# Attention and channel mix on one core: batch 5's output transposed by DMA, two tail loads moved ahead of a weight, fewer filler matmuls, and new written-out orders

## The chip, the cores and the metric

The kernel runs on one core of a Trainium2 chip. Its time is that of one execution on the device in microseconds (us), the median of three runs: 228.89 us before the change (228.83 to 229.37). The engines are named as in the profile: PE is TensorE's matmuls and PEld its weight loads, DVE is VectorE, ACT is ScalarE, POOL is GpSimd and SP is SyncE. POOL and SP issue transfers here, and POOL's convert float32 to bfloat16 on the way.

## The reference

Two layers follow each other. The first is causal attention with a linear distance bias and a window of 128 tokens, for 8 batches, 8 heads, 576 tokens and a head size of 64. The second mixes each token with the one before it and applies a gated, squared-ReLU feed-forward with 512 features and 1024 hidden ones.

```python
# attention, per batch and head
scores = q @ k.T / sqrt(64)
mask = (rel >= 0) & (rel < 128)            # rel = query position - key position
attn = softmax(where(mask, scores - slope[h] * |rel|, -1e9))
x[:, heads side by side] = attn @ v
# channel mix
xk = mu_k * x + (1 - mu_k) * x_prev        # x_prev: the token before
xr = mu_r * x + (1 - mu_r) * x_prev
out = sigmoid(xr @ w_r) * ((relu(xk @ w_k) ** 2) @ w_v)
```

## The kernel before

**Attention.** The work is cut by batch `b` (0 to 7) and by group `g` of two heads (0 to 3). q and k must stand with the head dimension on the partitions. For batches 0 to 3 PE transposes them through PSUM, and ACT or DVE copies the result to `qk` (`qk_quad`, `qk_some`). For batches 4 to 7 (`XB`) SP issues eight transposing DMAs per batch, `qx<-cb` (`flip`). The 64 tokens behind the last full block of 128 are the tail: q's and k's go to `ts` and, transposed, to `tt`; v's go to `tv`. Scores (`scores`) are matmuls over 64 rows, with the two heads side by side in the array. Batch 0 adds the bias by a matmul of `sid` and `dist`; later batches multiply by `mask` on DVE. ACT takes the exponential into `at`. The value product (`attend`) multiplies `at` by `vs` and `tv`, whose extra column of ones gives the sum; DVE divides (`rc`) and writes `xu`.

**From attention to channel mix.** `xu` has tokens on the partitions and must be turned. PE turns it in batches 0 to 5. In batch 0 it does so by group (`out_t`). In batches 1 to 5 (`OH`) it does so for two groups at once (`out_some`): 20 small transposes into two PSUM banks, copied by ACT to `xt`. For the batches in `XO` SP issues a transposing DMA per group instead, `xt<-xu` (`out_flip`); `XO` is asked first. DVE then takes the difference of neighbouring tokens (`dl`) and makes `xk` and `xr` (`shift`).

**Channel mix.** Two batches make 1152 tokens, worked in chunks of 256, 384 or 512 (`channel_mix`). Per chunk there are eight groups of four matmuls with `wk_sb`, with ReLU on ACT and the square on DVE or ACT (`kk`). Per 128 tokens come four matmuls with `wr_sb` and a tanh on ACT (`rs`), then eight with `wv_sb`, and DVE writes `ot`, which has five buffers, and SP stores it. All matmuls are recorded at one line, L395.

**What sets the order.** A planner (`Plan`) makes a node of each piece of work. For PE, ACT and DVE the table `ORDER` says which node takes which place, so an engine runs exactly the written list and waits where a node isn't ready. SP's and POOL's orders come from the planner's modelled run. POOL loads follow `LOADS`, a string of steps: `v` and `V` are batch 0's v (blocks 0 and 1; blocks 2, 3 and the tail), `2` its second half of q and k, `t` its tails of q and k, `K` and `k` the halves of w_k, `a`, `b`, `c` batch 1, `R` w_r, `W` and `w` the halves of w_v. At the start PE runs `NWARM` matmuls of a zeroed tile (`warm`, the fillers), which also stand in the list between pieces of batch 0. The last stores are cut in two where a count of SP's and ACT's transfers, `n_hw`, isn't a multiple of 8 (`n_split`).

Of the kernel before, what the change touches and what calls it, by code (L numbers as in the profile page):

```python
# [20 lines left out]

ORDER = {
    "PE": [int(x) for x in """
# [17 lines left out]
""".split()],  # L41
    "ACT": [int(x) for x in """
# [11 lines left out]
""".split()],  # L54
    "DVE": [int(x) for x in """
# [16 lines left out]
""".split()],  # L72
}

# [168 lines left out]
def kernel(  # L243
# [14 lines left out]
    B, H, S, D = q.shape  # L258
# [15 lines left out]
    PE, ACT, DVE, POOL, SPE, FAB, VIR = "PE", "ACT", "DVE", "POOL", "SP", "FAB", "VIR"  # L274
    NQ, NA, NX, NV, NC = 4, 4, 4, 2, 2
    XB = range(4, B)
    XO = range(6, B)
    X0 = 16
    NWARM = 90
    LOADS = 'v2KtVkabRWwc'  # L280
    XD = 4
    OTL = 1.5
    FIN = 384
# [328 lines left out]
    def load_step(what):  # L612
        if what in "vV":
            if what == "v" and VCUT:
                n_w["d"] = pool_op(0.55, emit_cut, [n_ident])
            for j in ((0, 1) if what == "v" else (2, 3)):
                vl[0].append(v_load(0, j, vh[0], [gv[0]] + blank_v + (
                    src0[1, VDEP - 1] if VDEP and j == 0 else [])))
                if j == 0 and not VCUT:
                    n_w["d"] = pool_op(0.55, emit_cut, [n_ident, last[POOL]])  # L620
                    last[POOL] = n_w["d"]
            if what == "V":
                vl[0].append(tv_load(0, vh[0], blank[0:4]))
        elif what in "23":
            if what == "2":
                src1[0] = src1[1] = [run_load(lambda: part_buf, i, 0, 256, 2, 0, H) for i in range(2)]
        elif what == "t":
            th[0], tl[0] = tail_load(0)
        elif what in "Kk":
            j = int(what == "k")  # L630
            n_w["k", j] = w_load(wk_sb[:, :, 512 * j:512 * j + 512],
                                 moe_w_k[:, 512 * j:512 * j + 512], 820 + 210 * (1 - j))
        elif what == "R":
            n_w["r"] = w_load(wr_sb, moe_w_r, 840)
        elif what in "Ww":
            j = int(what == "w")
            n_w["v", j] = w_load(wv_sb[:, 4 * j:4 * j + 4], moe_w_v[512 * j:512 * j + 512], 820)
        elif what in "abc":
            batch_load(1, what)
# [33 lines left out]

    for what in LOADS:
        load_step(what)
# [32 lines left out]
    g_wm = plan.add(VIR, 0.0001, 0.0001, [], (0,), None, [h_wm])  # L708
    for i in range(NWARM):
        plan.add(PE, 0.118 if i < 40 else 0.056, 0.0, [n_warm, g_wm], (1e12, i), emit_warm, (), [h_wm])  # L710
# [277 lines left out]

    n_hw = 39 + sum(4 if g in FT else 2 for g in range(3)) + 8 * len(XB) + len(XTT) + G * len(XO)
    n_split = -n_hw % 8  # L990
# [249 lines left out]
    for b in range(1, B):  # L1240
# [4 lines left out]
        for g in range(G):  # L1245
# [21 lines left out]
            r, hx = attend(b, g, 0, NJ, ha, [m0, m1] + vl[b], prio)  # L1267
            if b in XO:
                xks[b, g], xrs[b, g] = shift(b, g, 0, S, out_flip(b, g, r, hx, xth[b]),
# [54 lines left out]
```

## Time and profile before

| | |
|---|---|
| median of three runs | 228.89 us |
| the profiled execution | 228.23 us |
| its span (first to last instruction) | 226.2 us |
| granted TensorE clock | 0.998 |
| PE busy | 218.4 us, 2572 matmuls |
| DVE busy | 186.3 us |
| ACT busy | 156.2 us |
| POOL busy | 92.1 us |

The span is about 2.0 us shorter than the execution, whose start and end lie around it. In a row of the timeline the first number is the start in us from the span's beginning, the second the length of the merged piece, then come engine, line, operation, output<-input by the program's names, shapes and a count. In brackets stands how long the engine had been idle, and what ended that. A PE piece is as long as its matmuls' pipelined ends are modelled, so rates are read from start to start. Rows of DMA issues (SPq, POOL) show the issue; the landing comes later and is told as "to landing".

### The profile page before, as it was taken

How to read it: one execution, taken by the hardware profiler on the slowest of the kernel's cores; microseconds unless marked ns; L12 is line 12 of the kernel's file. 1: busy time of each engine (PE TensorE's matmuls, PEld its weight loads, DVE VectorE, ACT ScalarE, POOL GpSimd, SP SyncE). 2: the span in 40 equal slices, each digit the busy share in tenths (PEclk: the TensorE clock that was granted, in tenths of full speed). 3: DMA queues.
4: the chain of work that ended last, by engine and by line, in shares of the span. 5: the costliest groups of instructions: out<-in, count | busy, mean ns of one | idle time of the engine just before them, and what ended most of it. 6: DMA issues, size and time to landing. Idle time of an engine off the chain costs nothing.

```text
span 226.2 us, 6452 instructions
## 1 busy us (share of the span) xinstructions
PE 218.4 (97%) x2572; PEld 132.6 (59%) x2603; DVE 186.3 (82%) x418; ACT 156.2 (69%) x284; POOL 92.1 (41%) x118
## 2 busy tenths in 40 slices
PE   8999999999999999999999999999999999999994
PEld 7766855756666555555666554556665564655442
DVE  7388979899879999988989969969989999834153
ACT  2489999899999876877497198665697644545121
POOL 8956727599971973396258610330000000000000
PEclk9999999999999999999999999999999999999999
DMA  6999999999999999999999999799811083202026
GB/s 169 180 185 199 197 195 177 224 149 155 182 171 165 98 194 173 197 170 151 206 183 128 155 188 179 155 114 239 154 31 32 36 158 64 90 3 80 17 96 229
DMA packets 129981, 33.19 MB, mean 147 GB/s; under 512 B 116632, under 2 KB 126112, under 8 KB 129952
## 3 DMA queue, kind: packets, MB, share of 16 engines
q0 software_dynamic: 95728, 16.26, 100.6%
q1 hardware_dynamic: 32480, 15.94, 33.5%
q10 hardware_dynamic: 1744, 0.59, 1.1%
q8 instruction: 20, 0.33, 0.6%
q14 instruction: 9, 0.07, 0.1%
HBM read 33.56 MB, written 9.44 MB: 190 GB/s over the span
## 4 chain that ended last, share of the span: by engine, by line
PE 78%; ACT 12%; DMA 3%; DVE 3%; issue 2%; DVEq 0%; ACTq 0%
PE duo L395 68%; PE duo L742 6%; ACT at L766 3%; PE duo L398 3%; DMA out_dram<-ot 3%; ACT qk L715 3%; ACT xt L715 2%; ACT rl L1022 2%; ACT mask L1198 1%; DVE ot L1054 1%; PE duo L748 1%; ACT kk L994 1%; DVE xu L819 1%; DVE kk L996 0%; ACT rs L1040 0%
## 5 line engine op out<-in xcount | busy, mean ns | idle before, releaser
L395 PE MATMUL duo<-xk,wk_sb 128*128 128x256 bf16 (+2 forms) x413 | 71.0, 313 | 0.5 <-ACT rl L1022 0.2
L766 ACT ACTIVATE at<-duo 128x1024 bf16<-128x1024 f32 (+2 forms) x68 | 64.4, 1008 | 8.4 <-PE duo L742 8.3
L395 PE MATMUL duo<-wv_sb,kk 128*128 128x512 bf16 (+2 forms) x279 | 68.5, 373 | 1.3 <-issue 0.6
L1022 ACT ACTIVATE rl<-duo 128x256 bf16<-128x256 f32 (+2 forms) x104 | 47.6, 499 | 26.2 <-PE duo L395 20.9
L395 PEld LDWEIGHTS <-wk_sb 128*128 128x128 bf16 x416 | 38.9, 97 | 23.8 <-issue 1.6
L779 DVE TENSOR_TENSOR at<-at,mask 128x1024 bf16<-128x1024 bf16 x56 | 37.9, 686 | 7.1 <-ACT at L766 6.7
L395 PEld LDWEIGHTS <-kk 128*128 128x128 bf16 x296 | 26.8, 98 | 27.4 <-issue 0.9
L519 POOL DMA_DIRECT2D vs<-in_v_dram x32 | 28.5, 909 | 32.5 <-PE duo L395 30.9
L996 DVE TENSOR_TENSOR kk<-rl 128x256 bf16<-128x256 bf16 (+2 forms) x92 | 29.6, 336 | 10.8 <-ACT rl L1022 10.1
L1040 ACT ACTIVATE rs<-duo 128x512 bf16<-128x512 f32 x36 | 22.3, 628 | 22.5 <-DVE ot L1054 15.1
L395 PE MATMUL duo<-wr_sb,xr 128*128 128x512 bf16 x133 | 34.9, 379 | 0.6
L1054 DVE SCALAR_TENSOR_TENSOR ot<-rs,duo 128x512 f32<-128x512 bf16 (+2 forms) x37 | 24.3, 664 | 9.3 <-PE duo L395 5.7
L819 DVE TENSOR_TENSOR xu<-duo,rc 128x640 bf16<-128x640 f32 (+2 forms) x36 | 26.6, 745 | 0.4
L913 DVE SCALAR_TENSOR_TENSOR xr<-dl,mu_sb,xt 128x576 bf16<-128x576 bf16 (+1 forms) x32 | 24.9, 779 | 0.0
L913 DVE SCALAR_TENSOR_TENSOR xk<-dl,mu_sb,xt 128x576 bf16<-128x576 bf16 (+1 forms) x32 | 24.5, 778 | 0.1
L395 PEld LDWEIGHTS <-at 128*128 128x128 bf16 x576 | 21.3, 97 | 5.5 <-issue 0.9
L395 PEld LDWEIGHTS <-xr 128*128 128x128 bf16 x144 | 13.8, 98 | 14.5 <-issue 0.4
L395 PE MATMUL duo<-vs,at 128*128 128x65 bf16 x512 | 21.8, 193 | 0.0
L550 POOL DMA_DIRECT2D cb<-in_k_dram x20 | 17.8, 930 | 4.9 <-DMA vs<-in_v_dram 4.4
L550 POOL DMA_DIRECT2D cb<-in_q_dram x20 | 17.8, 942 | 1.4 <-DMA cb<-in_k_dram 1.4
L715 ACT COPY xt<-duo 128x640 bf16<-128x640 bf16 (+3 forms) x28 | 15.6, 593 | 2.4 <-PE duo L398 2.4
L715 ACT COPY qk<-duo 128x512 bf16<-128x512 bf16 (+1 forms) x26 | 15.1, 605 | 2.6 <-PE duo L398 2.6
(73 smaller groups left out, 189.0 us busy)
## 6 DMA issues: line engine op xcount, KB each, us to landing
out_dram<-ot SPq DMA_DIRECT2D x30, 256.0 KB, 4.7
vs<-in_v_dram POOLq DMA_DIRECT2D x32, 128.0 KB, 7.9
cb<-in_q_dram POOLq DMA_DIRECT2D x20, 128.0 KB, 9.5
cb<-in_k_dram POOLq DMA_DIRECT2D x20, 128.0 KB, 10.8
out_dram<-ot SPq DMA_DIRECT2D x10, 128.0 KB, 1.8
wk_sb<-in_moe_w_k_dram POOLq DMA_DIRECT2D x2, 512.0 KB, 8.7
cb<-in_q_dram POOLq DMA_DIRECT2D x4, 256.0 KB, 8.7
cb<-in_k_dram POOLq DMA_DIRECT2D x4, 256.0 KB, 8.9
```

Source lines behind the costliest of these rows:

```text
L395: return use(h, nc.tensor.matmul(*a, **k))
L519: return dma(POOL, 256, issue_t(1024), lambda e: nc.gpsimd.dma_start(out=vs_buf[h.idx][:, j, :, 0:D], in_=v[b, :, 128 * j:128 * j + 128].r ...
L550: return [dma(POOL, 256, issue_t(1024), lambda e, r=r: nc.gpsimd.dma_start(out=cb_buf[h.idx][:, i, r], in_=src[:, :, r]), [g], kind="q") f ...
L715: return (nc.scalar.copy if e == ACT else nc.vector.tensor_copy)(out=out, in_=in_)
L766: lambda e, ah=ah, w=w, hp=hp: nc.scalar.activation(out=ah(), in_=two(hp)[:, :, 0:w], func=AF.Exp, scale=float(scale)), (), [hp])
L779: nc.vector.tensor_tensor(out=a, in0=a, in1=m, op=ALU.mult)
L819: use(hp, nc.vector.tensor_tensor(out=out_, in0=a5()[:, :, :, 0:D], in1=rc[:, :, 0:nt, None].to_broadcast([128, 2, nt, D]), op=ALU.mult), hx)
L913: lambda e: nc.vector.scalar_tensor_tensor(out=buf[hk.idx][:, g, e0 + c0:e0 + c1], in0=dls(), scalar=mu[:, g:g + 1], in1=xc(1), op0=ALU.mu ...
L996: nc.vector.tensor_tensor(out=out, in0=in_, in1=in_, op=ALU.mult)
L1022: a = op(ACT, act_t(n), [s], pr, lambda e, hp=hp, hr=hr: use(hp, nc.scalar.activation(out=rl_buf[hr.idx][:, 0:n], in_=one(hp)[:, 0:n], fun ...
L1040: lambda e, hp=hp, hs=hs: use(hp, nc.scalar.activation(out=rs_buf[hs.idx], in_=one(hp), func=AF.Tanh, scale=0.5), hs), [hs], [hp])
L1054: use(hv, nc.vector.scalar_tensor_tensor(out=ot_buf[ho.idx][:, a:b], in0=rs_buf[hs.idx][:, a:b], scalar=1.0, in1=one(hv)[:, a:b], op0=ALU. ...
```

## The change

`XO` takes batch 5 in, so that its four groups are turned by four transposing DMAs from SP, and 40 small transposes on PE and four copies on ACT are no longer there. The step `t` stands ahead of `K`. `NWARM` is 82 instead of 90. `n_hw` rises by four, so that one late store is cut in two instead of five. The lists for PE, ACT and DVE are new from end to end; of them only the beginnings are shown.

```diff
 ORDER = {
     "PE": [int(x) for x in """
-40 113 74 125 85 56 118 80 117 109 43 51 42 89 121 63 103 88 49 92 96 66 94 48 119 127 126 68 100 55 101 110 107
...
+84 109 92 74 83 70 64 40 43 115 97 106 59 80 62 102 110 47 81 100 50 65 105 91 117 103 60 77 93 49 79 112 72 63
...
     XB = range(4, B)
-    XO = range(6, B)
+    XO = range(5, B)
     X0 = 16
-    NWARM = 90
-    LOADS = 'v2KtVkabRWwc'
+    NWARM = 82
+    LOADS = 'v2tKVkabRWwc'
     XD = 4
```

Three places show what moves. The first is ACT at the start, behind its four loads of k (`qk_71`, `qk_74`, `qk_73` and `qk_72` hold batch 0's groups 0, 1, 2 and 3; COPY and CAST to `qk` bring transposed q and k out of PSUM, ACTIVATE to `at` is the exponential). Before:

```order
L715 ACT_TABLE_LOAD
L715 COPY qk_71<-duo_126 128x2x256
L766 ACTIVATE at_77<-duo_124 128x2x384
L715 CAST qk_73<-duo_126 128x2x256
L766 ACTIVATE at_78<-duo_123 128x2x384
L715 COPY qk_74<-duo_126 128x2x256
L766 ACTIVATE at_78<-duo_125 128x2x384
L715 COPY qk_74<-duo_123 128x2x128
```

Now:

```order
L766 ACT_TABLE_LOAD
L766 ACTIVATE at_77<-duo_124 128x2x384
L715 CAST qk_73<-duo_124 128x2x256
L766 ACTIVATE at_78<-duo_123 128x2x384
L766 ACTIVATE at_79<-duo_124 128x2x384
L766 ACTIVATE at_77<-duo_125 128x2x384
L715 COPY qk_72<-duo_124 128x2x128
L715 COPY xt_89<-duo_123 128x256
```

Two of the three 256-wide copies have left ACT (they stand in DVE's list now), and the four exponentials follow each other with one copy among them.

The second is POOL's loads of batch 0: `qx_75` is the second half of q and k, `wk_sb` the first half of w_k, `ts_67` the tails, `vs_63` and `tv_65` v.

```order
 L515 DMA qx_75<-in_q_dram 128x8x128
 L515 DMA qx_75<-in_k_dram 128x8x128
-L560 DMA wk_sb<-in_moe_w_k_dram 128x4x512
 L534 DMA ts_67<-in_q_dram 128x1x256
 L534 DMA ts_67<-in_k_dram 128x1x256
+L560 DMA wk_sb<-in_moe_w_k_dram 128x4x512
 L519 DMA vs_63<-in_v_dram 128x8x64 x2
 L524 DMA tv_65<-in_v_dram 64x8x64
```

The half of w_k has moved behind both tails; every other load keeps its place.

The third is SP where batch 6's eight q and k transposes (`qx_75<-cb_62`) are issued, up to the first of batch 7 (`qx_76<-cb_61`). Before:

```order
L554 DMA_TRANSPOSE qx_75<-cb_62 128x4x128 x8
L1079 DMA out_dram<-ot_107 128x512
L1079 DMA out_dram<-ot_108 128x512
L647 DMA_TRANSPOSE tt_69<-ts_67 128x4x128
L1079 DMA out_dram<-ot_109 128x512
L1079 DMA out_dram<-ot_110 128x512
L554 DMA_TRANSPOSE qx_76<-cb_61 128x4x128 x3
```

Now:

```order
L554 DMA_TRANSPOSE qx_75<-cb_62 128x4x128 x8
L1079 DMA out_dram<-ot_107 128x512
L647 DMA_TRANSPOSE tt_69<-ts_67 128x4x128
L928 DMA_TRANSPOSE xt_90<-xu_85 128x5x128
L1079 DMA out_dram<-ot_108 128x512
L928 DMA_TRANSPOSE xt_90<-xu_86 128x5x128
L928 DMA_TRANSPOSE xt_90<-xu_88 128x5x128
L928 DMA_TRANSPOSE xt_90<-xu_87 128x5x128
L1079 DMA out_dram<-ot_107 128x512
L554 DMA_TRANSPOSE qx_76<-cb_61 128x4x128 x3
```

Four transposes of batch 5's `xu` stand between batch 6's and batch 7's, with one store among them, and a store less stands there than before.

86 rows, old and new, of the table ORDER are left out of this document.

## The prediction

> **What bounds the kernel now.** I read the page's busy times first, then the busy times of five stretches of the span, then TensorE's timeline row by row.
>
> ```profile
> PE 218.4 (97%) x2572; PEld 132.6 (59%) x2603; DVE 186.3 (82%) x418; ACT 156.2 (69%) x284; POOL 92.1 (41%) x118
> ...
> 16.00:30.00 14.00, 13.30 (x290) 10.11 (x288) 13.19 (x38) 14.00 (x39) 8.98 (x13) 1.00 1.42 199
> 30.00:80.00 50.00, 49.24 (x770) 30.70 (x777) 44.72 (x91) 47.41 (x89) 36.41 (x45) 1.00 1.90 167
> 80.00:130.00 50.00, 49.20 (x537) 28.96 (x543) 46.23 (x95) 34.00 (x57) 29.74 (x36) 1.00 2.01 173
> 130.00:180.00 50.00, 49.22 (x483) 28.21 (x490) 44.80 (x90) 35.94 (x57) 4.88 (x6) 1.00 1.07 124
> 180.00:222.00 42.00, 41.68 (x261) 22.37 (x266) 26.38 (x56) 16.31 (x34) 0.00 (x0) 1.00 0.31 82
> ```
>
> The stretches give PE, PEld, DVE, ACT and POOL busy, then the granted clock. From 30 us on TensorE idles 0.76 + 0.80 + 0.78 + 0.32 = 2.7 us in 192. Before that ACT is full (14.00 of 14) and DVE nearly (13.19). A busy PE need not be at its peak, so the starts are compared:
>
> ```profile
> 131.33 0.47 PE L398 MATMUL duo<-ident,xu 64*128 64x64 bf16 x20
> 131.63 0.79 PE L742 MATMUL duo<-qx 64*128 64x256 bf16 x12
> ...
> 135.21 1.89 PE L395 MATMUL duo<-xk,wk_sb 128*128 128x512 bf16 x8
> 136.94 1.03 PE L395 MATMUL duo<-wr_sb,xr 128*128 128x512 bf16 x4
> ...
> 147.50 0.47 PE L398 MATMUL duo<-ident,xu 64*128 64x64 bf16 x20
> 147.80 0.55 PE L742 MATMUL duo<-qx 64*128 64x256 bf16 x8
> ```
>
> Eight matmuls of 512 columns take 136.94 - 135.21 = 1.73 us, 216 ns each, and the next work starts at once. So there are two regimes: a start set by ACT, DVE and landing data, then a stream in which each microsecond of TensorE work is one of the kernel. An edit counts if it takes work from the stream or lets the stream start earlier.
>
> **Batch 5's transposes.** The same rows are those that leave: 20 + 20 small transposes, 131.63 - 131.33 and 147.80 - 147.50, 0.30 us each. Both stand next to scores in the same 64-row mode, so no change of mode goes with them. They lie in the stream: **-0.60 us**. With them four ACT copies go, which cost nothing, as ACT is busy 35.94 of 50 us there.
>
> What replaces them is four transposing DMAs on SP:
>
> ```profile
> qx<-cb SPq DMA_TRANSPOSE x32, 7.5
> xt<-xu SPq DMA_TRANSPOSE x8, 3.1
> ...
> L906 DVE TENSOR_TENSOR dl<-xt x7: 450/453/455, 163.6 to 190.4; 128x576 bf16<-128x576 bf16 x7
> L913 DVE SCALAR_TENSOR_TENSOR xk<-dl,mu_sb,xt x8: 809/812/820, 154.6 to 191.5; 128x576 bf16<-128x576 bf16 x8
> ```
>
> The DMA rows end in the count and the median us from issue to landing: 7.5 among the loads, 3.1 when they are over. Batch 5's lie among loads, so I take 7.5. In the new TensorE order, between batch 5's last value product and the first 384-column product that reads its result, there stand 18 groups of four 512-column matmuls (18 x 4 x 0.216 = 15.6 us), eight scores and one value product: 18 us together. The result's way takes about 1 us to the issue, 7.5 to land, 0.45 and 0.81 on DVE: 10 us. Margin 8 us, so cost 0 (by 3.1 us the margin is 12; the other end is a landing twice as late, 15 us, which the margin just covers). Each of the four waits on SP for DVE's `xu`. Behind them in SP's queue stand stores, which have five buffers, and batch 7's transposes, whose first scores stand over 5 us of work nearer to the end than before; nothing there is short of time. If the margin went, each microsecond late would be one of the stream.
>
> **The start.** The first transposes of batch 0 stood behind 57 fillers and three bias products, now behind 46 fillers:
>
> ```profile
> 0.99 3.32 PE L395 MATMUL duo<-warm 128*128 128x128 bf16 x34 [0.99 <-DVE warm L488]
> 4.15 1.14 PE L748 MATMUL duo<-dist,sid 128*128 128x384 bf16 x6
> 5.12 1.45 PE L395 MATMUL duo<-warm 128*128 128x128 bf16 x23
> 6.41 0.39 PE L398 MATMUL duo<-ident,qx 128*128 128x128 bf16 x4
> ...
> 3.59 0.73 DVE L715 CAST qx<-qx 128x256 bf16<-128x256 f32 x1
> ...
> 6.83 0.58 ACT L715 COPY qk<-duo 128x512 bf16<-128x512 bf16 x1 [2.64 <-PE duo L398]
> 7.85 0.81 ACT L766 ACTIVATE at<-duo 128x768 bf16<-128x768 f32 x1 [0.43 <-PE duo L742]
> 8.51 0.69 DVE L715 CAST qk<-duo 128x512 bf16<-128x512 f32 x1 [1.44 <-PE duo L398]
> ```
>
> Their data is cast at 3.59 + 0.73 = 4.32, yet they start at 6.41. The first 34 fillers take 4.15 - 0.99 = 3.16 us (93 ns each), the next 23 take 6.41 - 5.12 = 1.29 (56 ns). So 46 end at 0.99 + 3.16 + 12 x 0.056 = 4.82: 1.6 us earlier. The copy behind them moves from ACT (0.58) to DVE (0.69), so its result comes at 4.82 + 0.22 + 0.2 + 0.69 = 5.9 (a transposing group and a handover of about 0.2 each, as between 6.41, 6.83 and the rows' lengths), where it was ready at 6.83 + 0.58 = 7.4, and the first exponential, at 7.85, can come some 1.1 to 1.5 us earlier. What is late next on ACT is the second exponential, which waits for data still landing. The eight fewer fillers (0.45 us) fill waits and count as nothing beside this.
>
> How much reaches the stream is capped by a transfer:
>
> ```profile
> L560 POOL DMA_DIRECT2D wr_sb<-in_moe_w_r_dram x1: 811/811/811, 18.1 to 18.1; - x1
> DMA to landing us min/median/max: 11.2/11.2/11.2
> ...
> 30.09 1.89 PE L395 MATMUL duo<-wr_sb,xr 128*128 128x512 bf16 x7
> ...
> 34.60 0.45 PE L398 MATMUL duo<-ident,cb 64*64 64x64 bf16 x32
> 34.97 0.39 PE L742 MATMUL duo<-qk 64*128 64x256 bf16 x4
> ```
>
> w_r lands at 18.1 + 11.2 = 29.3 and is first used at 30.09. Its place among the loads is unchanged, so the new program cannot use it before 29.3: at most 0.8 us earlier. The work ahead of that point is the same in both lists, but for the fillers and one more group of 32 transposes (34.97 - 34.60 = 0.37 us), which moves from behind it to ahead of it. Cap: 0.8 + 0.37, about 1.2 us. The other end is a loss: ACT and DVE are full until 30 us, and orders that reach them worse could cost as much, say +1.0. I take **-0.80**: nearer the cap, as the 1.1 to 1.5 us gained at the first exponential exceed the 0.8 that the transfer lets through, and two of three 512-wide copies leave ACT, which has no slack there.
>
> **The load order.** Two tail loads pass the first half of w_k on POOL (the change's words also name v, but v and w_k keep their order):
>
> ```profile
> 5.98 0.77 POOL L560 DMA_DIRECT2D wk_sb<-in_moe_w_k_dram x1
> 6.72 0.56 POOL L534 DMA_DIRECT2D ts<-in_q_dram x1
> ...
> DMA to landing us min/median/max: 8.3/8.7/9.1
> L395 PE MATMUL duo<-ident,ts x32: 221/234/237, 16.8 to 17.2; 64*64 64x32 bf16 x32
> L395 PE MATMUL duo<-xk,wk_sb x40: 269/272/283, 21.4 to 30.0; 128*128 128x256 bf16 x40
> ```
>
> The first row now stands behind the two tail issues (0.56 us each; the second is like the first). w_k goes out 1.1 us later and lands by 5.98 + 9.1 + 1.1 = 16.2 at the latest; its first use is at 21.4. The tails, 0.8 us earlier, are read at 16.8, which the order of work sets. Both hidden: 0, within 0.3 either way.
>
> **The stream's waits and the end.** New lists put the 2.7 us of idle time elsewhere. Both lists have nearly the same changes of row mode behind w_r's first use (58, were 59). I take 0; a quarter gone gives -0.7, a doubling +2.7. At the end SP issues four fewer half stores:
>
> ```profile
> 218.69 4.84 SPq L1079 DMA_DIRECT2D out_dram<-ot  x8
> 222.61 0.75 DVE L1054 SCALAR_TENSOR_TENSOR ot<-rs,duo 128x384 f32<-128x384 bf16 x2 [0.88 <-ACT rs L1040]
> ```
>
> The last store waits for DVE at 222.61, not for the queue: 0.
>
> **Sum.** -0.60 - 0.80 = -1.4 us. The profiled execution took 228.23 (span 226.2 and 2.0 around it), 0.66 under the median of 228.89; I put the difference on the median: **227.5**.
>
> **Rivals.** *The start gives nothing* (DVE at 13.19 of 14 is the bound, and two 0.69 us copies were added to it): only the transposes remain, 228.89 - 0.60 = 228.3, no change by a measurement of this kernel (0.3%, 0.7 us). For it: DVE gets work from ACT; against: that work lies before 12 us, where DVE waited 1.44 us for one copy alone.
>
> *Slower: batch 4's scores wait for SP.*
>
> ```profile
> 76.48 2.16 SPq L554 DMA_TRANSPOSE qx<-cb  x1
> ...
> 79.51 2.74 SPq L554 DMA_TRANSPOSE qx<-cb  x2
> ...
> 85.13 5.50 SPq L1079 DMA_DIRECT2D out_dram<-ot  x2
> 91.21 0.83 PE L742 MATMUL duo<-qx 64*128 64x256 bf16 x12
> ```
>
> The last two of batch 4's eight transposes are issued by 79.51 + 2.74 = 82.25 and, at 7.5 us, land at 89.8; the scores start at 91.21. Now three of the eight stand behind the second store instead of two, 1.4 us more of issuing. If the store itself comes 1.4 us earlier with the whole stream, the landing stays at 89.8, and so does TensorE's arrival, 91.21 - 1.4: no margin is left. SP takes its queue in order: at 85.13 two stores cost it 5.5 us. If a store held these transposes for as long, the stall would be 5.5 us: 233.0. The result turns slower from a stall of 2.1 us on. Against it: the store's matmuls stand no later in the new list, and 7.5 is a median, not the time of these two.
>
> *The clock falls.* The PE clock was 1.00 in every stretch above, after a start in which fillers took 93 instead of 56 ns. Were fewer fillers to let it fall for as long as at the start, 3.16 x (1 - 56/93) = 1.3 us would be lost: 228.8. The Trainium skill, TensorE: Matmul & The Clock Gate, "What's actually happening", says the clock is released by a busy window of about 3.4 us and falls after an idle one. By that rule no idle time here is long enough, the clock stays, and the sum is still 227.5. The rows show no fall either; so a small chance.
>
> *More than forecast:* the stream's waits shrink too, 226.8.
>
> **How the numbers follow.** Forecast 0.50, more than forecast 0.10: faster 0.60. Start gives nothing 0.18 and clock 0.03: same 0.21. Slower, by SP or by doubled waits, 0.19. The likeliest case's own range is 226.9 to 228.1. Low end: -0.60 - 1.2 - 0.7 = 226.4. High end: no gain at the start and half of the doubling on top, 229.7; the rest of the slower cases lie beyond, under 2 in 10 with what lies below.
>
> **What would show it.** First L398 transposes near 4.8 and first exponential near 6.5 us; w_r's first use near 29.4, at its landing; no `ident,xu` rows between 125 and 150, and four more `xt<-xu` transposes landing in 5 to 8 us; TensorE idle after 30 us about 2.7 us. Wrong, if w_r's first use is not earlier than 30, or a wait of over 1 us for `qx` or for ACT and DVE stands in the stream.

## The result, and the profile after

The changed kernel takes 226.99 us (median of four runs, 226.97 to 227.05) where the kernel before took 228.86 us beside it: a ratio of 0.9913, with a 95% interval from 0.9892 to 0.9934. That is 1.87 us less. Timed once more later, it took 227.45 against 229.07 us, a ratio of 0.9933 (0.9909 to 0.9957). Its profiled execution took 226.97 us with a span of 225.1; that of the kernel before took 228.23 with 226.2. So the two profiles differ by 1.26 us, and the medians by more. Where the other 0.6 us is, is the main thing that the experiments showed. Of the 1.26, 1.1 lie in the span. The rest lies outside: in all executions with the old start the time is 2.0 us longer than the span, in those of the changed kernel 1.9. Why is open.

The stretches of the changed kernel, with PE, PEld, DVE, ACT and POOL busy, the granted clock, DMA share and GB/s:

```profile
16.00:30.00 14.00, 13.32 (x332) 10.32 (x331) 12.85 (x39) 13.23 (x34) 8.69 (x12) 1.00 1.42 198
30.00:80.00 50.00, 49.14 (x739) 30.74 (x747) 44.13 (x91) 46.95 (x88) 36.07 (x44) 1.00 1.97 172
80.00:130.00 50.00, 49.53 (x539) 28.66 (x546) 46.73 (x93) 37.97 (x61) 26.34 (x32) 1.00 1.80 165
130.00:180.00 50.00, 49.47 (x451) 27.91 (x455) 43.36 (x90) 30.62 (x51) 8.19 (x10) 1.00 1.21 151
180.00:221.00 41.00, 40.79 (x259) 21.93 (x262) 27.96 (x61) 16.01 (x34) 0.00 (x0) 1.00 0.25 78
```

ACT has become free at the start (13.23 of 14 us, was full), but TensorE did not get ahead by that. Its timeline and those of DVE and ACT at the start:

```profile
0.99 4.53 PE L395 MATMUL duo<-warm 128*128 128x128 bf16 x46 [0.99 <-DVE warm L488]
5.36 0.39 PE L398 MATMUL duo<-ident,qx 128*128 128x128 bf16 x4
5.97 0.67 DVE L715 COPY qk<-duo 128x512 bf16<-128x512 bf16 x1
7.43 0.81 ACT L766 ACTIVATE at<-duo 128x768 bf16<-128x768 f32 x1 [3.19 <-PE duo L742]
...
30.37 1.02 PE L395 MATMUL duo<-wr_sb,xr 128*128 128x512 bf16 x3
```

The first transposes start at 5.36 (6.41 before), the first exponential at 7.43 (7.85 before), but the first product with w_r at 30.37 (30.09 before), behind 0.37 us of transposes that moved ahead of it. So next to nothing of the early start arrives there. And w_r was not what it waited for:

```profile
L560 POOL DMA_DIRECT2D wr_sb<-in_moe_w_r_dram x1: 768/768/768, 17.8 to 17.8; - x1
DMA to landing us min/median/max: 11.0/11.0/11.0
```

It landed at 17.8 + 11.0 = 28.8, 1.6 us ahead of its use.

For the stream I compared starts of the same work. A value product of batches 2 and 3 at 79.2 us is a place up to which both written lists hold the same pieces, but for fillers. The row of TensorE's timeline before:

```profile
79.24 1.04 PE L395 MATMUL duo<-wv_sb,kk 128*128 128x512 bf16 x4
```

and the changed kernel's, with its last row of `ot`:

```profile
79.23 1.90 PE L395 MATMUL duo<-wv_sb,kk 128*128 128x512 bf16 x8
...
221.48 0.75 DVE L1054 SCALAR_TENSOR_TENSOR ot<-rs,duo 128x384 f32<-128x384 bf16 x2 [0.89 <-PE duo L395]
```

At 79.2 us the two profiled executions are level. The last `ot` comes at 221.48 instead of 222.61: 1.13 us are won behind that place. The two transposing groups explain some 0.5 of them (0.60, if all their work counts; `a_dup` below shows four fifths). The other 0.5 to 0.6 must be small waits that the new order of batches 4 to 7 avoids; I found no single wait of over 0.35 us there in either trace, so this part is a difference, not something that a row shows.

Batch 5's transposing DMAs were hidden. The first row is of the DMA issues in 130:142 (count, median us to landing), the others of the timeline:

```profile
xt<-xu SPq DMA_TRANSPOSE x4, 8.7
```

```profile
146.65 0.45 DVE L906 TENSOR_TENSOR dl<-xt 128x576 bf16<-128x576 bf16 x1
...
152.86 0.45 DVE L906 TENSOR_TENSOR dl<-xt 128x576 bf16<-128x576 bf16 x1
154.62 1.63 PE L395 MATMUL duo<-xk,wk_sb 128*128 128x384 bf16 x9
```

The last of the four was issued at 139.69 and landed at 148.21. DVE reads the four results from 146.65 on and the last at 152.86, and TensorE needs what DVE makes of them at 154.62.

### The profile page after: what moved, and what is told of

The parts are those of the page before. It is cut to its first block, busy times and chain, and to the rows that moved or that the text cites. A ratio compares the mean times of both kernels' runs of the same rounds, so it can differ in the third digit from the quotient of the medians.

```text
span 225.1 us, 6344 instructions
## 1 busy us (share of the span) xinstructions
PE 217.7 (97%) x2525; PEld 131.5 (58%) x2555; DVE 186.8 (83%) x422; ACT 153.0 (68%) x276; POOL 91.9 (41%) x118
## 4 chain that ended last, share of the span: by engine, by line
PE 91%; ACT 4%; DVE 2%; issue 1%; DVEq 0%
PE duo L395 77%; PE duo L742 7%; PE duo L398 4%; PE duo L748 2%; ACT at L766 1%; ACT xt L715 1%; ACT rl L1022 1%; ACT qk L715 1%; DVE ot L1054 1%; DVE qk L715 1%; ACT kk L994 0%; DVE at L779 0%; ACT rs L1040 0%; DVE tv L499 0%; DVE tt L715 0%
## 5 line engine op out<-in xcount | busy, mean ns | idle before, releaser
L395 PE MATMUL duo<-xk,wk_sb 128*128 128x256 bf16 (+2 forms) x410 | 70.2, 312 | 0.3
L395 PE MATMUL duo<-wv_sb,kk 128*128 128x512 bf16 (+2 forms) x281 | 66.1, 373 | 1.1 <-issue 0.5
L779 DVE TENSOR_TENSOR at<-at,mask 128x1024 bf16<-128x1024 bf16 x56 | 37.2, 680 | 5.8 <-ACT at L766 5.7
L395 PE MATMUL duo<-wr_sb,xr 128*128 128x512 bf16 x135 | 35.5, 379 | 0.5
L1040 ACT ACTIVATE rs<-duo 128x512 bf16<-128x512 f32 x36 | 21.6, 612 | 19.8 <-PE duo L395 17.1
L395 PEld LDWEIGHTS <-xr 128*128 128x128 bf16 x144 | 13.3, 98 | 12.9 <-issue 0.4
L550 POOL DMA_DIRECT2D cb<-in_k_dram x20 | 17.8, 926 | 7.3 <-DMA vs<-in_v_dram 7.2
L715 ACT COPY qk<-duo 128x512 bf16<-128x512 bf16 (+1 forms) x25 | 14.5, 593 | 0.4 <-PE duo L398 0.4
L906 DVE TENSOR_TENSOR dl<-xt 128x576 bf16<-128x576 bf16 (+1 forms) x32 | 13.4, 438 | 1.1 <-ACT xt L715 0.6
```

The source lines that it names most:

```text
L395: return use(h, nc.tensor.matmul(*a, **k))
L550: return [dma(POOL, 256, issue_t(1024), lambda e, r=r: nc.gpsimd.dma_start(out=cb_buf[h.idx][:, i, r], in_=src[:, :, r]), [g], kind="q") f ...
L715: return (nc.scalar.copy if e == ACT else nc.vector.tensor_copy)(out=out, in_=in_)
L779: nc.vector.tensor_tensor(out=a, in0=a, in1=m, op=ALU.mult)
L1040: lambda e, hp=hp, hs=hs: use(hp, nc.scalar.activation(out=rs_buf[hs.idx], in_=one(hp), func=AF.Tanh, scale=0.5), hs), [hs], [hp])
```

## The experiments

Two theories stood against each other. **A** is the prediction's: the start gives some 0.8 us up to w_r's landing, the transposes 0.6, the rest nothing. **B** is what the traces suggested in its place and took shape over the first runs: the start of the kernel before differs from execution to execution, and this difference is what the new start removes.

Nearly every run changes one thing in one of the two kernels. The table `ORDER` was written out again wherever pieces of work move or go. Where it says "buffers as in" a kernel, a second table holds every piece of work to the buffer and PSUM bank that it has there, since otherwise the planner deals them out anew.

### The old and the new start exchanged

Everything up to the first product with w_r comes from the other kernel's lists, with its fillers and load order; behind that the kernel's own lists.

```diff
 # a_oldstart: the changed kernel
-    NWARM = 82
-    LOADS = 'v2tKVkabRWwc'
+    NWARM = 90
+    LOADS = 'v2KtVkabRWwc'
 # b_newstart: the kernel before
-    NWARM = 90
-    LOADS = 'v2KtVkabRWwc'
+    NWARM = 82
+    LOADS = 'v2tKVkabRWwc'
```

> The changed kernel with the old start: 90 fillers, the old load order, and on TensorE, ACT and DVE everything that the kernel before does up to the first product with w_r stands in the old order; behind that the new lists. Theory A: the start was worth 0.80 us: 227.8 us. Theory B: the start brought nothing into the stream (the first product with w_r starts at 30.37 us in the changed kernel, 30.09 before, with 0.37 us of transposes moved ahead of it): 227.0 us, within 0.2.

> The kernel before with the new start: 82 fillers, the new load order, and everything up to the first product with w_r in the new order; behind that the old lists, with batch 5's transposes on TensorE. Theory A: 228.86 - 0.80 = 228.1 us. Theory B: 228.9 us, within 0.3.

Measured: 230.56 and 231.57 us (before: 229.14), both far from either theory. The joint itself costs that much: waits of 0.2 to 0.6 us, most of them for ACT, stand between 30 and 55 us, probably because the pieces of batch 1 that one list had done were not those that the other supposes; from 57 us on little more is lost. Row of a_oldstart's timeline with the longest:

```profile
35.54 0.40 PE L738 MATMUL duo<-qk 64*128 64x256 bf16 x4 [0.62 <-ACT rs L1036]
```

The totals say nothing on the start. But a_oldstart has the old start up to 30 us, and there TensorE's pieces come 0.63 us later than in the profile before, from the first to the last. That was the first sign that one list has more than one start.

### Batch 5 by DMA in the old lists, by TensorE in the new ones

```diff
 # b_xo5: the kernel before
-    XO = range(6, B)
+    XO = range(5, B)
 # a_xo6: the changed kernel
-    XO = range(5, B)
+    XO = range(6, B)
```

In b_xo5 the transposes and copies are struck from the lists. In a_xo6 the two transposing groups stand ahead of batch 6's scores, and the copies among its exponentials.

> The kernel before with batch 5's output turned by four transposing DMAs; the 40 transposes and four copies are struck from its lists, and nothing else is moved. Theory A, if the old lists leave the DMAs as much room as the new ones: 228.86 - 0.6 = 228.3 us. Theory B: about 227.5 us. Theory D: the old lists leave no room, since batch 5's last xu is ready at 146.5 us there, its DMA lands some 8.5 us after its issue, so near 156, and the products that read it start at 156.3 with two DVE steps still between: a stall of 1.5 to 3 us, so 229.5 to 231.5 us, and the new lists are what makes the DMAs pay.

> The changed kernel with batch 5's output turned by TensorE again: 40 small transposes stand beside batch 6's scores, four copies in ACT's list; fillers, load order and every other place of the lists as in the changed kernel. Theory A (the prediction): the two transposing groups are worth 2 x 0.30 us of the stream, the copies nothing: 226.99 + 0.6 = 227.6 us. Theory B (read from the two traces afterwards: the start gained nothing, and TensorE's waits are shorter only from 130 us on, where batch 5's transposes and copies stood): this part carries nearly the whole gain, 228.2 to 228.9 us. Theory C: the DMA's own cost eats the gain: 227.0 us or less.

Measured: b_xo5 234.02 us, slower by 2.06% (1.74 to 2.38), which is theory D, and more than it priced; a_xo6 232.73, slower by 1.64% (1.39 to 1.88), more than all theories. Where b_xo5 loses, on DVE and TensorE:

```profile
141.11 0.46 DVE L902 TENSOR_TENSOR dl<-xt 128x576 bf16<-128x576 bf16 x1 [4.58 <-DMA xt<-xu]
145.53 0.37 PE L391 MATMUL duo<-vs,at 128*128 128x65 bf16 x7 [1.90 <-ACT rs L1036]
147.73 0.42 PE L391 MATMUL duo<-vs,at 128*128 128x65 bf16 x8 [1.83 <-DVE at L775]
...
159.69 0.46 DVE L902 TENSOR_TENSOR dl<-xt 128x576 bf16<-128x576 bf16 x1 [1.56 <-DMA xt<-xu]
```

DVE's list has batch 5's `dl` where the copies used to be ready. Now it stands 4.58 us for a landing, the squares and masks behind it come late, and TensorE waits twice for 1.9 us. The new lists put batch 5's value products some 10 us earlier (132.6 and 134.0 for groups 2 and 3, were 143.1 and 144.5) and DVE's `dl` of these groups behind the landing. The DMA is free only with that.

In a_xo6 it is the other way round:

```profile
140.10 0.40 PE L739 MATMUL duo<-qx 64*128 64x256 bf16 x4 [0.46 <-ACT xt L712]
141.03 0.39 PE L739 MATMUL duo<-qx 64*128 64x256 bf16 x4 [0.53 <-ACT at L763]
...
146.22 0.40 PE L739 MATMUL duo<-qx 64*128 64x256 bf16 x4 [1.26 <-ACT at L763]
...
173.50 0.39 PE L739 MATMUL duo<-qx 64*128 64x256 bf16 x4 [0.90 <-ACT at L763]
...
178.03 0.34 PE L739 MATMUL duo<-qx 64*128 64x256 bf16 x4 [0.89 <-ACT at L763]
```

The copies on ACT delay the exponentials, and scores wait for the PSUM banks. The waits at 173 and 178 us, far from the edit, come where 96 pieces of work had got other buffers. So neither run prices the transposes alone; they show that a part of this change without its lists makes the kernel 4.9 and 3.6 us slower than the kernel before.

### What a microsecond of TensorE's work in the stream is worth

Since the transposes could not be priced by putting them back, I added work of a known length where they would have stood: the first score products of batch 6 done twice.

```diff
-            for (pieces, m0, tt, a0, w, hp) in todo:
+            for (pieces, m0, tt, a0, w, hp) in todo * (2 if b == 6 and todo[0][1] == 0 else 1):
```

> The changed kernel with the first score products of batch 6 done twice (four groups of four 256-column products, 0.225 us each in its trace, written over with the same values), with lists and buffers as they are. Theory A (behind w_r TensorE is the bound, and work taken out counts one for one, on which the 0.60 us of batch 5's transposes rest): 4 x 0.225 = 0.9 us more than the changed kernel on this chip. Rival: the added work falls into TensorE's waits, of which 0.5 us lie between 130 and 180 us: 0.4 to 0.5 us more.

Measured: 228.07 us (on that chip the kernel before 229.07, the changed one 227.45), 0.6 us more by medians of times that scatter over about 1 us. The traces are sharper. The changed kernel's three score groups, and the same in a_dup:

```profile
138.66 0.83 PE L742 MATMUL duo<-qx 64*128 64x256 bf16 x12
139.42 2.76 PE L395 MATMUL duo<-wv_sb,kk 128*128 128x512 bf16 x12
```

```profile
138.73 1.48 PE L742 MATMUL duo<-qx 64*128 64x256 bf16 x24
140.14 2.76 PE L395 MATMUL duo<-wv_sb,kk 128*128 128x512 bf16 x12
```

TensorE is 0.07 us late when it arrives and 0.72 when it leaves; after the fourth group it is 0.79 late and stays so to the end. Of 0.90 us added 0.72 arrive: four fifths, between the two expectations and nearer A. Taken over to the transposes, 0.60 us of work are worth about 0.5, an estimate.

### Fillers at the start

```diff
 # b_less11: the kernel before, 11 of the 57 leading fillers less, buffers as before
-    NWARM = 90
+    NWARM = 79
 # a_less20, a_more20: the changed kernel, 26 or 66 leading fillers for 46, its buffers
-    NWARM = 82
+    NWARM = 62        # a_more20: 102
```

> The kernel before with 11 of the 57 fillers ahead of the first transposes struck (79 fillers in all), every other place and every buffer as in the kernel before. Theory A (the prediction: the start reaches the stream): 11 x 0.056 = 0.6 us less, 228.3 us. Theory B (read from the traces so far: the old start is late by half of how long the fillers keep their slow pace, which ends at another moment in each execution, 3.6 to 5.7 us after the span's start, and this lateness reaches the end unchanged): also about -0.6 us at the median, and the spread of about 1 us from execution to execution stays. Theory C (data or ACT and DVE bound the start): 228.9 us.

> The changed kernel with 20 of the 46 leading fillers struck, every other place and every buffer as it is. The first transposes can then start when their data is cast, near 4.7 us instead of 5.36. Theory A: the whole 0.6 us reaches the end, 226.4 us. Theory B: the new start no longer hangs on TensorE there (in the run with batch 5's transposes put back the first transposes came 0.44 us earlier, and nothing of it was left at 9.1 us): 227.0 us, within 0.15.

> The changed kernel with 20 more fillers ahead of the first transposes, every other place and every buffer as it is; they take 20 x 0.056 = 1.1 us at the fast pace. Theory A: 228.1 us. Theory B: some of it is absorbed, as the start has at least 0.4 us of room: 227.3 to 227.7 us. Theory C: all of it is absorbed: 227.0 us.

> The changed kernel as it is, beside the other runs of this chip. Theory B (read from ten traces: the fillers' slow pace ends 3.6 to 6.5 us after the span's start, differently in each execution; the old start pays half a microsecond for each microsecond beyond 3.7, the new one only beyond 5.1, and neither gets below a floor that both share): most executions lie at 227.0 us, a part up to 0.7 above it, median 227.0 to 227.4 us, and the kernel before, on the same chip, 228.2 to 229.7 us with its median 1.7 to 2.2 above. Theory A: a fixed gain, both with a spread alike, and a difference of 1.4 us.

Measured: b_less11 229.01 us where the kernel before took 229.36 on that chip (ratio 0.9997, 0.9971 to 1.0023), which decides nothing, as the 0.6 us that A and B both expected lie just inside the interval; a_less20 227.67 (0.9929, 0.9902 to 0.9956), a_more20 228.20 (0.9952, 0.9929 to 0.9975); the changed kernel again 227.45, from 226.99 to 227.83, beside 229.07, from 228.36 to 230.28. That difference of 1.6 us lies between A's 1.4 and B's 1.7 to 2.2, so the totals of a_again do not tell the two apart. Against the kernel before on their chip, a_less20 is 1.7 us faster (A expected 2.5, B 1.9) and a_more20 1.2 (A 0.8, B 1.2 to 1.6), both nearer B. The times of b_less11 spread as widely as those of the kernel before, from 228.08 to 230.67 us. With fewer fillers ahead of the data they should spread less by what follows, and this stays unexplained.

What sets the times apart is seen in the fillers themselves. Here are stretches of 1 us with the fillers alone (PE busy and their count, a filler that reaches in included; granted clock, DMA). First the kernel before, then the same old start in b_xo5:

```profile
3.00:4.00 1.00, 1.00 (x15) 1.00 1.10 305
```

```profile
3.00:4.00 1.00, 1.00 (x12) 1.00 1.07 306
4.00:5.00 1.00, 0.80 (x8) 1.00 0.80 182
```

and the changed kernel in its first profile and in the repeat:

```profile
3.00:4.00 1.00, 1.00 (x12) 1.00 1.07 286
4.00:5.00 1.00, 1.00 (x14) 1.00 1.03 233
5.00:6.00 1.00, 0.94 (x18) 1.00 1.51 204
```

```profile
4.00:5.00 1.00, 1.00 (x12) 1.00 1.05 230
5.00:6.00 1.00, 1.00 (x11) 1.00 1.50 191
```

A filler takes either 107 ns from start to start or 56, and the change from one to the other is sharp: at most one filler lies between there. It came at 3.6 us in the profile before, at 4.7 in the profile after, and at 6.9 in the repeat (each the start of the piece in which it falls). Until then all of TensorE's work is about twice as long. The granted clock reads 1.00 throughout, so that column doesn't show it. The Trainium skill, TensorE: Matmul & The Clock Gate, "What's actually happening", says that the clock is released by a busy window of about 3.4 us which runs freely, so that the moment varies, by 500 ns either way. That the moment varies is seen here, but by far more: the ends that I found, 3.6 to 6.9 us, lie 3.3 us apart, nearly one such window. In the profile before it came 2.6 us behind the first filler (at 0.99), sooner than a whole window. That the clock is what sets the pace is the page's statement; no column here shows it.

This is what it does to the start, read from the timelines: the end of the slow pace, the landing of the last part of batch 0's first k, and the first product with w_k. In each table the lateness counts from the profile of that kernel, before or after; the times of the two tables cannot be compared, since the new list has less work ahead of that product.

| old start | slow pace ends | k lands | first `xk,wk_sb` | later by |
|---|---|---|---|---|
| before | 3.6 | 7.7 | 21.40 | 0 |
| b_less11, 11 fillers fewer | 3.9 | 8.1 | 21.50 | 0.10 |
| a_oldstart | 4.9 | 8.0 | 22.04 | 0.64 |
| b_xo5 | 5.6 | 8.3 | 22.39 | 0.99 |

| new start | slow pace ends | k lands | first `xk,wk_sb` | later by |
|---|---|---|---|---|
| a_xo6 | 3.9 | 8.0 | 20.80 | 0.11 |
| a_loads, old load order | 4.3 | 8.2 | 21.02 | 0.33 |
| after | 4.7 | 7.9 | 20.69 | 0 |
| a_sid, a step on DVE moved | 4.7 | 8.4 | 20.88 | 0.19 |
| a_dup | 4.8 | 7.8 | 20.75 | 0.06 |
| b_newstart | 5.3 | 7.7 | 20.76 | 0.07 |
| a_loads_split | 5.8 | 8.0 | 21.01 | 0.32 |
| a_again | 6.9 | 7.9 | 21.56 | 0.87 |
| a_less20, 20 fillers fewer | 6.4 | 8.5 | 21.45 | 0.76 |
| a_more20, 20 more | 6.5 | 7.4 | 22.44 | 1.75 |

The old start loses half a microsecond for each that the slow pace lasts beyond 3.6; the new one only beyond about 5.15 (0.87 = 0.5 x (6.9 - 5.15)). The old start's lateness is there before k lands: the first transposes start at 7.03 in a_oldstart and 7.40 in b_xo5, 0.62 and 0.99 us later than before. Under these limits both stand on a floor, and the floor moves with the landing: in a_loads the slow pace ended early, but k landed 0.4 us later than in the profile after, and the product came 0.33 later. The lateness is kept: a_again is 0.88 us behind the changed kernel's first profile at 40 us and 0.87 at 218. The profile before was an execution on the floor (228.23 us; of 74 single times of that kernel beside the runs here, 3 are lower, and the slowest is 230.28). That is why it is 0.66 under the median, and why the two profiles are level at 79 us though the medians are not.

If the end of the slow pace is spread evenly over 3.55 to 6.95 us, the ends found with 0.05 us on either side, the old start loses 0.83 us on average and the new one 0.24, an estimate from these two lines: 0.6 us won at the start, 0.78 where the pace changes late and nothing where it changes early. 0.6 and the 1.26 between the two profiles make 1.86. Measured were 1.87, with all four executions of the changed kernel within 0.1 us of the floor, and 1.62 in the repeat.

What the floor is made of shows where 20 fillers are gone:

```profile
4.18 0.69 PE L434 MATMUL duo<-ident,qx 128*128 128x128 bf16 x4 [0.23 <-DVE qx L751]
...
7.04 0.34 PE L778 MATMUL duo<-qk 64*128 64x256 bf16 x4
...
8.20 0.64 PE L434 MATMUL duo<-id,qx 128*128 128x128 f32 x3 [0.29 <-DMA qx<-in_q_dram]
```

The first scores stand at 7.04, as early as in the changed kernel's first profile (7.05), though the slow pace lasted to 6.4. Then TensorE waits for the third part of q and k, which lands 0.6 us later than there. So fewer fillers did take out the lateness by pace in this execution, as theory B had not expected, and a landing held it instead. Another 0.2 us is lost by 20.6 us, for which I have no row.

### The step on DVE next to that

```diff
 # a_sid: DVE's list of the changed kernel, its buffers
-MEMSET tv 64x520
 TENSOR_SCALAR sid (fifth head)
 MEMSET at
 COPY qk 128x512
+MEMSET tv 64x520
```

> The changed kernel with one step of DVE's list moved: the 0.49 us clearing of a tv buffer at 9.16 us goes behind the copy of q and k that stands at 9.85, so that the last head's sid, for which TensorE waits at 10.10 us, is made at 9.16. All buffers as they are. Theory E (the floor of the start is DVE's chain at 8.3 to 10.1 us): up to 0.49 us earlier, 226.5 to 226.8 us, the median of the changed kernel on this chip less 0.3 to 0.5. Theory F (the floor is set by batch 1's q and k, which land at 25.2 us, or by ACT): no gain, within 0.15 us.

Measured: 227.11 us beside 227.45 for the changed kernel on that chip, both against 229.07 (ratios 0.9922 and 0.9933, intervals over each other). In its trace k lands 0.58 us later than in the profile after, TensorE is 0.49 late at 9.6 us, and 0.06 late at the product with this `sid`, at 10.16; 0.19 us remain. So the step gains some 0.4 us there, as theory E says, against a late landing that was chance. The median is the lowest of that chip, but whether it beats the changed kernel is not settled.

### Load order and stores

```diff
 # a_loads, and the first line of a_loads_split: the changed kernel, its buffers
-    LOADS = 'v2tKVkabRWwc'
+    LOADS = 'v2KtVkabRWwc'
-    n_hw = 39 + ... + G * len(XO)
+    n_hw = 39 + ... + G * (len(XO) - 1)
```

> The changed kernel with the old load order (the first half of w_k ahead of the tails of q and k) and five late stores cut in two instead of one; all else, buffers too, as in the changed kernel. Theories A and B both: 227.0 us, within 0.2: the tails land near 14.9 instead of 12.6 us and are first read at 16.0, and the last store waits for DVE. Theory D: the new start is tied to the tails' earlier landing, and their later one pushes batch 0's second half back by up to 1 us: 227.5 to 228 us.

> The changed kernel with the old load order alone (the first half of w_k ahead of the tails of q and k); stores, lists and buffers as in the changed kernel. In the run that also had the old stores, TensorE lost 0.48 us between 22 and 30 us in two waits with no releaser, each ended some 1.3 us behind an instruction fetch that came up to 1.4 us later than in the changed kernel, and nothing from there to the end. Theory G (the load order makes those fetches late): the same loss again, 0.3 to 0.6 us between 22 and 30 us in its trace, and a median 1.1 to 1.4 us under the kernel before, where the changed kernel is 1.6 under it. Theory H (chance of one execution): no such waits, and 1.5 to 1.9 us under the kernel before.

Measured: a_loads_split 228.07 beside 229.36, 1.3 us under the kernel before; a_loads 227.52 beside 229.45, 1.9 under it. a_loads_split's trace has two waits without a releaser, and that of a_loads has one, shown behind them:

```profile
22.98 0.60 PE L432 MATMUL duo<-xk,wk_sb 128*128 128x256 bf16 x4 [0.30 <-issue]
...
29.18 0.32 PE L435 MATMUL duo<-ident,cb 64*64 64x64 bf16 x17 [1.10 <-issue]
```

```profile
28.66 0.32 PE L435 MATMUL duo<-ident,cb 64*64 64x64 bf16 x17 [0.70 <-issue]
```

a_loads lacks the first wait. The second it has, ahead of the same transposes, and so has the changed kernel's own profile, with 0.20 us. In a_loads it costs nothing that lasts: TensorE is 0.33 us late at 25 us and 0.33 at 35, and its median lies where the changed kernel's does. So theory H holds for the time, the load order is worth nothing measurable, but not for the waits, of which only the first was of that execution.

Inside the span the stores are worth nothing either: a_loads_split is 0.80 us late at 35 us and 0.79 at 220, with all five stores cut in two. Outside it this run loses: its executions are 2.3 us longer than their spans on average, those of a_loads and the changed kernel 1.9, some 0.4 us, most of what a_loads_split is slower by. Its number of transfers is no longer a multiple of 8, as it is in both kernels, so it does not stand for the old stores, and whether that is the cause was not tested. In a_xo6 and b_newstart, which have five stores cut and the count a multiple of 8, it is 1.9.

## Why the prediction was right, and where not

The time, 226.99, lies 0.5 under the forecast and inside the range, and the direction is right. Of the terms, not all are, and that the sum came so near is in part luck: between the two profiles the start gave nothing of its 0.80, and the stream's waits, put at 0, gave 0.5 to 0.6 in its place.

**Batch 5's transposes, -0.60.** Right in kind and nearly in size: 0.72 of 0.90 us of like work arrive at the end, so some 0.5 of the 0.60. The DMAs took 8.7 us to land where I took 7.5, and the way to the last issue took 3.7 us (from 136.0 to 139.69, behind two others on SP) where I took 1. So the margin was some 5 us, not 8, and it held. That it held was the new lists' doing; with the old ones the rival "each microsecond late would be one of the stream" came true at 5 us.

**The start, -0.80.** The size is near the 0.6 us that the start gives on average, by luck, for the reason was wrong in each step. By the prediction's own sign it failed: w_r's first use was to come before 30 us, and it came at 30.37. "The first 34 fillers take 93 ns each" was a mean over two paces, of an execution in which the slow one happened to end early; the 46 fillers end at 5.36, not at 4.82. The 0.4 us gained at the first exponential did not arrive at all. And w_r was no cap: it was there 1.6 us before its use in the profile after. What failed is the step from an earlier first exponential to an earlier stream. In its place: both starts have a floor, which leaves the two profiles level at 79 us and moves with the landing of q and k and with what DVE does next, and they differ in how long the slow pace may last before TensorE falls behind it.

**The median.** "I put the difference on the median" treated 0.66 us as an offset that both kernels have. It was the usual lateness of the old start, and a third of the gain. That step is why 227.5 is too high.

**The stream's waits, 0.** About 0.5 to 0.6 us less behind 79 us, none before. The range allowed for -0.7. The idle time of the stretches from which I took 2.7 us is no measure for so little: the repeat of the changed kernel shows in 80:130

```profile
80.00:130.00 50.00, 50.00 (x539) 28.50 (x535) 46.70 (x94) 38.24 (x61) 25.77 (x32) 1.00 1.95 166
```

50.00 us busy where its first profile has 49.53, with the same 539 matmuls, while its lateness stays at 0.88 us throughout.

**The load order, 0,** and **the end, 0.** Right within what was measured: a_loads; and from the last `ot` to the end of the span it is 3.6 us before and after. The 0.1 us outside the span stands in no term.

**The rivals.** Batch 4's scores did not wait: they start at 91.25 us (91.21 before). The pace of TensorE, which had 0.03 as "the clock falls", was what mattered most for the start, with the other sign: fewer fillers ahead of real work lose less while it is slow. "The start gives nothing" is what the two profiles alone would have said.

## What to carry to other kernels

A profile is one execution: where its time is off the median, look for the place where executions differ before the difference is carried along as an offset. Work at the head of a program is priced at the slow pace and for the whole spread of its end; a filler ahead of real work is cheap only if it is over when the data are there. In a program whose order and buffers are written out, a single part taken over without the rest can cost several times what it is worth, so hold the buffers fixed when one part is to be priced.

## What the runs showed that I had not expected

The slow pace ended at 3.6 to 6.9 us in executions of like programs. Behind the start, executions repeat: the lateness of a_more20 against the changed kernel is 1.75 us at 20 us and 1.75 at 221, so that a trace tells 0.1 us where the times of six to twelve executions scatter by about 1. And TensorE stood without a releaser for 0.3 and 1.1 us in a_loads_split. In the trace's packets a fetch of instructions ends 1.3 and 1.5 us ahead of the two resumptions (21.70 and 27.69 us), and one ends at 26.49 in the changed kernel, 1.3 us ahead of a resumption at 27.82. The same wait, from 0.20 to 1.10 us long, stands in seven of the profiles, and in each it ends 1.3 to 1.5 us behind the end of such a fetch. That TensorE waited there for its own instructions fits these times, and no run tests it.
